# Four tokens of q and k per partition, permuted PSUM reads and contiguous writes in a chunked attention and wave-MLP kernel

## The chip, the cores and the metric

The kernel runs on one core of one Trainium2 chip. The core has five engines that run side by side: TensorE (PE in the profile, with its weight loads as PEld), VectorE (DVE), ScalarE (ACT), GpSimd (POOL, which here mostly issues loads) and SyncE (SP, which issues stores and transposing copies). Sixteen DMA engines move data between HBM and SBUF. The metric is the device time of one execution in microseconds; the time before is the median of 11 runs.

## The reference

q, k and v are 8 x 8 x 576 x 64 (batch, heads, tokens, head size). Attention is computed in chunks of 64 tokens; its output, with the heads side by side, is the input x (8 x 576 x 512) of a second phase.

```python
def attention(q, k, v):
    scores = scale * matmul(q_c, k_c.transpose(...))      # per chunk of 64 tokens
    attn = softmax(scores)
    out = matmul(attn, v_c)
    return out.reshape(B, H, S, D)

def wave_mlp(x, w_theta, w_tok_r, w_tok_i, w_ch):
    theta = x @ w_theta
    zr, zi = x * cos(theta), x * sin(theta)
    y = einsum('ts,bsd->btd', w_tok_r, zr) + einsum('ts,bsd->btd', w_tok_i, zi)
    u = x + y
    return u + maximum(u @ w_ch, 0.0)
```

## The kernel before

The eight batch rows are taken as four pairs of 1152 tokens, that is nine blocks of 128 tokens. A pair's blocks form five groups, `GROUPS` = (0,2), (2,2), (4,1), (5,2), (7,2): first block and number of blocks n. Group 2, the middle one, holds 64 tokens of either batch row; the other four are "large" (n = 2, 256 tokens) here and the middle one "small". All arithmetic is in fp16 with fp32 in PSUM; the loads convert from fp32.

There is no loop nest. `ORDER` is a list of items such as `a1.0.2:3`, written out by hand or by a planner, and the program walks it: the item's name picks a function, its numbers are pair, group and so on, and the number after the colon is a set of bits that choose engines and layouts. Each engine runs its instructions in the order in which this list produces them, and waits only on semaphores. The items are:

- `lq` (`load_qk`), `lv`, `lw`, `lt`, `lc`: loads, issued by POOL. Up to eight q/k tiles (`NAT`) are in flight or waiting. `lq` puts two tokens of a head side by side in a partition: a descriptor is 2 x 64 elements, 512 bytes in HBM and 256 in SBUF. A large group has 128 partitions x 8 heads of these for q and as many for k, in the same 128 partitions.
- `a1`: transposes q and k of a group on PE into one PSUM tile and copies q to `qT` and k to `kT` (`copy`, on ACT or DVE by bits 1 and 2). With bit 32 it uses 64 transposes of 64 rows, else 32 of 128 rows. The copies read PSUM in order; `kT` is written with its two tokens interleaved, so that keys stand in order of tokens.
- `a2`: scores, 64 x 64 each, on PE, then one exp on ACT that writes `eT` in order of query tokens, that is, every second element.
- `a3`: attention times v on PE, with the sums in a column of ones; reciprocal and product on DVE give x. `a4` transposes x (PE and a copy, or DMA with bit 16). `a5` is theta with its cosine and sine on ACT; `z` the products on DVE.
- `tw`: transposes of the token weights. `y`, `yh`: the token mixing, 18 matmuls and an addition on DVE. `ut`, `w`, `st`: the channel mixing, the final addition and the store, issued by SP or, with bit 2, by POOL.

PSUM holds four tiles of two banks each (`psum`, bufs=4), which all these stages share. `make_identity` is issued by POOL right after the first item. The transposes of `a1`, `a4` and `tw` need that identity.

Of the kernel before, what the change touches and what calls it, by code (L numbers as in the profile page):

```python
# [10 lines left out]
FP16 = mybir.dt.float16  # L11
# [5 lines left out]


ORDER = """
lq.0.0:0 lq.0.2:0 a1.0.0:35 a1.0.2:3 lq.0.1:0 a2.0.0:0 lv.0.2:0 a2.0.2:0 lv.0.0:0  # L20
a1.0.1:1 a3.0.2.0:0 a3.0.0.0:0 lw.0:0 lv.0.1:0 a3.0.0.1:0 a4.0.2:1 lq.0.3:0 a2.0.1:0
a4.0.0:33 a5.0.2:0 a3.0.1.0:0 a3.0.1.1:0 z.0.2.0:0 a5.0.0:0 lt.0.1:0 a4.0.1:33 a1.0.3:3
z.0.0.0:0 tw.0.0:1 lq.0.4:0 lt.1.0:0 tw.0.2:1 a5.0.1:0 lv.0.3:0 lt.1.1:0 z.0.0.1:0
lv.0.4:0 lq.1.0:0 z.0.1.0:0 z.0.1.1:0 lq.1.2:0 tw.0.1:1 a1.0.4:2 lq.1.1:0 a2.0.3:0
lv.1.2:0 tw.1.0:0 yh.0.0:0 a2.0.4:0 a3.0.3.0:0 lc.0:0 lv.1.0:0 a3.0.3.1:0 lq.1.3:0
yh.0.1:0 lq.1.4:0 tw.1.2:1 lv.1.1:0 lv.1.3:0 a4.0.3:1 lv.1.4:0 tw.1.1:1 a3.0.4.0:0
a3.0.4.1:0 a5.0.3:0 z.0.3.0:0 yh.1.0:0 a4.0.4:0 a1.1.0:1 a1.1.2:2 a5.0.4:0 z.0.3.1:0
lq.2.0:0 lq.2.2:0 z.0.4.0:0 yh.1.1:0 z.0.4.1:0 a2.1.2:0 a1.1.1:2 a2.1.0:0 w.0.0:0
lq.2.1:0 w.0.1:0 st.0.0:0 a2.1.1:0 st.0.1:0 y.0.1.0:0 a3.1.0.0:0 a3.1.2.0:0 a1.1.3:3
y.0.1.1:0 a4.1.2:0 a1.1.4:3 a2.1.3:0 a3.1.0.1:0 y.0.1.2:0 a3.1.1.0:0 a2.1.4:0 w.0.2:0  # L30
st.0.2:0 a5.1.2:0 a3.1.1.1:0 y.0.1.3:0 a4.1.1:0 a3.1.4.0:0 lv.2.3:0 a4.1.0:32 a1.2.0:35
w.0.3:0 z.1.2.0:0 a5.1.1:0 st.0.3:2 a3.1.3.0:0 a5.1.0:0 a3.1.4.1:0 lv.3.2:0 a1.2.2:2
a1.2.1:0 a3.1.3.1:0 a4.1.4:0 w.0.4:0 a4.1.3:0 lv.2.1:0 z.1.1.0:0 st.0.4:0 w.0.5:0
z.1.1.1:0 lq.2.3:0 z.1.0.0:0 a5.1.4:0 lv.2.0:0 w.0.6:0 st.0.5:2 z.1.0.1:0 a5.1.3:0
lq.2.4:0 lv.2.2:0 st.0.6:0 z.1.4.0:0 y.1.0.0:0 z.1.4.1:0 w.0.7:0 z.1.3.0:0 st.0.7:0
a1.2.3:35 a2.2.1:0 z.1.3.1:0 y.1.0.1:0 lq.3.0:0 w.0.8:0 lq.3.2:0 a2.2.0:0 st.0.8:2
lq.3.1:0 lv.2.4:0 lv.3.3:0 a2.2.2:0 y.1.0.2:0 a3.2.0.0:0 a3.2.2.0:0 y.1.0.3:0 a3.2.0.1:0
lv.3.4:0 a3.2.1.0:0 lq.3.3:0 y.1.1.0:0 a4.2.2:0 a2.2.3:0 a1.2.4:0 a3.2.1.1:0 w.1.0:0
lv.3.1:0 st.1.0:0 a5.2.2:0 a4.2.1:1 y.1.1.1:0 a4.2.0:32 a3.2.3.0:0 a1.3.0:35 a5.2.1:0
a1.3.2:2 z.2.2.0:0 lv.3.0:0 a3.2.3.1:0 a5.2.0:0 z.2.1.0:0 y.1.1.2:0 lq.3.4:0 a2.3.2:0  # L40
a2.2.4:0 z.2.0.0:0 z.2.1.1:0 a1.3.1:0 z.2.0.1:0 y.1.1.3:0 w.1.1:0 a3.2.4.0:0 st.1.1:0
ut.1.1.2:0 a3.3.2.0:0 y.2.0.0:0 a4.2.3:17 a2.3.0:0 a3.2.4.1:0 w.1.2:0 st.1.2:2 y.2.0.1:0
a2.3.1:0 a1.3.3:32 a4.2.4:16 a3.3.0.0:0 y.2.0.2:0 a2.3.3:0 a3.3.0.1:0 a1.3.4:35
y.2.0.3:0 a3.3.1.0:0 a2.3.4:0 ut.1.1.1:0 ut.1.1.0:0 ut.1.1.3:0 w.1.3:0 a5.2.3:0 w.1.4:0
w.1.5:0 st.1.3:2 st.1.4:2 st.1.5:2 a5.2.4:0 z.2.3.0:0 a3.3.1.1:0 z.2.4.0:0 w.1.6:0
z.2.3.1:0 a4.3.0:49 a5.3.0:0 ut.2.0.2:0 z.2.4.1:0 w.1.7:0 st.1.6:2 st.1.7:0 ut.2.0.1:0
y.2.1.0:0 a3.3.4.0:0 a4.3.2:51 a3.3.3.0:0 ut.2.0.3:0 y.2.1.1:0 ut.2.0.0:0 a3.3.4.1:0
a3.3.3.1:0 a4.3.1:49 y.2.1.2:0 w.1.8:0 st.1.8:0 a5.3.2:0 w.2.0:0 a4.3.3:17 st.2.0:2
y.2.1.3:0 a4.3.4:16 w.2.1:0 z.3.2.0:0 a5.3.1:0 z.3.0.0:0 st.2.1:0 w.2.2:0 z.3.0.1:0
st.2.2:2 ut.2.1.2:0 ut.2.1.3:0 z.3.1.0:0 ut.2.1.0:0 ut.2.1.1:0 a5.3.3:0 z.3.1.1:0  # L50
w.2.3:0 st.2.3:2 a5.3.4:0 z.3.3.0:0 y.3.0.0:0 z.3.4.0:0 z.3.3.1:0 w.2.4:0 st.2.4:0
y.3.0.1:0 ut.3.0.0:0 z.3.4.1:0 w.2.5:0 ut.3.0.1:0 y.3.0.2:0 w.2.6:0 st.2.5:2 ut.3.0.2:0
st.2.6:0 y.3.0.3:0 y.3.1.0:0 w.2.7:0 st.2.7:0 y.3.1.1:0 ut.3.0.3:0 w.2.8:0 st.2.8:2
y.3.1.2:0 y.3.1.3:0 ut.3.1.0:0 ut.3.1.1:0 w.3.0:0 w.3.1:0 st.3.0:2 st.3.1:2 w.3.2:0
w.3.3:0 w.3.4:0 st.3.2:2 ut.3.1.2:0 w.3.5:0 ut.3.1.3:0 st.3.3:0 w.3.6:0 st.3.4:0 w.3.7:0
st.3.5:0 st.3.6:2 w.3.8:0 st.3.7:0 st.3.8:0
""".split()


# [1 line left out]
def kernel(  # L61
# [11 lines left out]
    nc = tc.nc  # L73
    B, H, S, D = q.shape
    DM = H * D
    CH = 64
# [82 lines left out]

    def load_qk(p, g):  # L160

        j0, n = GROUPS[g]
        t = nat.tile([P, 2, H, 2, D], FP16, name="qk16")
        nats[p, g] = t
        for ti, ap in enumerate((q, k)):
            for pp, bb, s0, m in in_ranges(j0):
                m = n * m
                src = ap[2 * p + bb, :, s0 : s0 + m, :]
                nc.gpsimd.dma_start(  # L169
                    t[(pp // 2) : (pp // 2) + m // 2, ti].rearrange(  # L170
                        "p h t d -> p h (t d)"
                    ),
                    src.rearrange("h (p t) d -> p h (t d)", t=2),
                )

    def v_parts(p, g):
# [100 lines left out]
    def a1(p, g, bits):  # L277

        j0, n = GROUPS[g]
        ps = psum2("ps_qkT", FP16)  # L280
        if bits & 32:

            psv = ps.rearrange("p (r w e t s) -> p w e t r s", r=2, w=2, e=NE, t=2)
        else:
            psv = ps.rearrange("p (w e t r s) -> p w e t r s", w=2, e=NE, t=2, r=2)
        t = nats.pop((p, g))
        rows = n * CH
        step = CH if bits & 32 else rows
        for w in range(2):
            for e in range(NE):  # L290
                for tk in range(2):
                    for par in range(2):
                        for r0 in range(0, rows, step):
                            rs = slice(r0, r0 + step)
                            nc.tensor.transpose(  # L295
                                psv[par * D : par * D + D, w, e, tk,
                                    r0 // CH : (r0 + step) // CH, :],
                                t[rs, w, 2 * e + par, tk, :],
                                id16[rs, rs],
                            )  # L300

        qT = qkp.tile([P, NE, 2, P], FP16, name="qT")
        kT = qkp.tile([P, NE, P, 2], FP16, name="kT")
        st[p]["qkT"][g] = qT, kT
        copy(not bits & 1,
             qT[:, :, :, 0:rows].rearrange("p e t (r s) -> p e t r s", s=CH),
             psv[:, 0, :, :, 0:n])
        copy(bits & 2,
             kT[:, :, 0:rows, :].rearrange("p e (r s) t -> p e t r s", s=CH),
             psv[:, 1, :, :, 0:n])  # L310

    def a2(p, g):

        j0, n = GROUPS[g]
        qT, kT = st[p]["qkT"].pop(g)
        kT = kT.rearrange("p e s t -> p e (s t)")

        ps = psum2("ps_sT").rearrange("p (r x) -> p r x", r=2)[:, :, 0 : n * NE * CH]
# [1 line left out]
        for i in range(n):  # L320
            for e in range(NE):
                for par in range(2):
                    for kh in range(2):
# [1 line left out]
                        nc.tensor.matmul(  # L325
                            psv[kh * CH : kh * CH + CH, par, i, e, :],
                            kT[par * D : par * D + D, e, c0 : c0 + CH],
                            qT[par * D : par * D + D, e, :, c0 // 2 : (c0 + CH) // 2],
                        )

        eT = epool.tile([P, 2 * H * CH], FP16, name="eT")[:, 0 : n * H * CH]
        st[p]["eT"][g] = eT.rearrange("p (r i e c) -> p r i e c", r=2, i=n, e=NE)
        nc.scalar.activation(  # L333
            out=eT.rearrange("p (r b s t) -> p r b t s", r=2, s=CH // 2, t=2),
            in_=ps.rearrange("p r (b t s) -> p r b t s", s=CH // 2, t=2),
            func=AF.Exp,
            scale=scale,
        )

    def a3(p, g, hg):  # L340

# [302 lines left out]
```

## Time and profile before

| what | us |
|---|---|
| median of 11 runs | 204.22 |
| lowest, highest | 202.84, 205.14 |
| profiled execution | 204.0 |
| its span | 202.2 |
| PE busy in the span | 185.0 |
| DVE busy | 129.2 |
| ACT busy | 108.5 |
| POOL busy | 94.8 |

The profile shows one execution. Its own time, 204.0, is 1.8 us above the span, which runs from the first to the last instruction. Durations from it are set against this execution. In a group's line, the numbers after the count are the busy time, the mean of one instruction in ns and, after the bar, the idle time of the engine just before with what ended it. "128*64" on a PE line means that 128 rows and 64 columns of the array are used. PE's ends are modelled, so that starts of successive instructions tell more than its busy share.

### The profile page before, as it was taken

The page shows a single profiled execution, that of the slowest core. Times are in us where ns is not written, and L with a number is a line of the kernel's source. Part 1 is how long each engine was busy: PE and PEld are TensorE (multiplying, and loading weights), DVE is VectorE, ACT ScalarE, POOL GpSimd, SP SyncE. Part 2 cuts the span into 40 slices and gives each one's busy share as a digit, 9 for nine tenths or more (in the row PEclk, how much of TensorE's full clock was granted, in tenths as well). Part 3 has the DMA queues.
Part 4 walks back from the last instruction along what each step waited for, and adds up shares of the span by engine and source line. Part 5 has one row for each costly group of instructions (what it writes and reads, how often), then busy time and mean ns, then how long its engine had stood idle before and what let it go on. Part 6 is the DMA issues. An engine that isn't in the chain of part 4 may idle for free.

```text
span 202.2 us, 7044 instructions
## 1 busy us (share of the span) xinstructions
PE 185.0 (91%) x3142; PEld 124.5 (62%) x3142; DVE 129.2 (64%) x224; ACT 108.5 (54%) x114; POOL 94.8 (47%) x135
## 2 busy tenths in 40 slices
PE   0377999999999998999999899999999999999991
PEld 0265377776677746567777477775466646677640
DVE  1037669836777669667685887565868494544572
ACT  2068499499826877969159792665841265000000
POOL 7989639798596108994599620101310111011020
PEclk9999999999999999999999999999999999999999
DMA  6999999999999907999999992746744659482786
GB/s 144 165 162 171 187 194 167 177 180 173 171 220 175 167 16 103 123 219 210 227 154 153 156 161 63 146 86 92 206 140 99 182 144 198 100 160 79 156 276 216
DMA packets 102157, 31.96 MB, mean 158 GB/s; under 512 B 95792, under 2 KB 98480, under 8 KB 102128
## 3 DMA queue, kind: packets, MB, share of 16 engines
q0 software_dynamic: 78800, 20.70, 98.0%
q1 hardware_dynamic: 23328, 10.82, 23.0%
q8 instruction: 24, 0.39, 0.8%
q14 instruction: 5, 0.04, 0.1%
HBM read 33.06 MB, written 9.44 MB: 210 GB/s over the span
## 4 chain that ended last, share of the span: by engine, by line
PE 75%; ACT 8%; DMA 6%; DVE 6%; issue 2%; POOL 1%; DVEq 0%; POOLq 0%
PE ps_y L521 30%; PE ps_uw L560 15%; PE ps_theta L443 13%; PE ps_qkT L295 4%; PE ps_y L500 3%; DMA qk<-in_k_dram 3%; PE ps_x L354 3%; DMA v<-in_v_dram 2%; PE ps_sT L325 2%; PE ps_xT L417 2%; ACT qT L214 2%; DVE x L368 2%; DVE kT L212 2%; ACT eT L333 1%; ACT xT L214 1%
## 5 line engine op out<-in xcount | busy, mean ns | idle before, releaser
L521 PE MATMUL ps_y<-wT,z 128*128 128x288 f16 x448 | 59.6, 287 | 0.5 <-PE ps_theta L443 0.5
L521 PEld LDWEIGHTS <-z 128*128 128x128 f16 x448 | 42.4, 98 | 13.8 <-PE ps_theta L443 1.0
L598 POOL DMA_DIRECT2D out_dram<-o x18 | 9.9, 552 | 82.6 <-DVE o L589 49.4
L190 POOL DMA_DIRECT2D v<-in_v_dram x56 | 41.9, 771 | 10.6 <-DMA qk<-in_k_dram 6.1
L560 PE MATMUL ps_uw<-wch,uT 128*128 128x512 f16 (+1 forms) x148 | 37.6, 374 | 0.0
L529 DVE TENSOR_TENSOR uT<-ps_y,xT 128x576 f16<-128x576 f32 x28 | 21.2, 756 | 24.7 <-PE ps_y L521 24.7
L443 PE MATMUL ps_theta<-wtheta,xT 128*128 128x512 f16 x128 | 31.7, 393 | 0.1
L453 ACT ACTIVATE cos<-ps_theta,pihalf 128x1024 f16<-128x1024 f32 (+1 forms) x20 | 20.6, 1029 | 16.5 <-PE ps_theta L443 14.7
L333 ACT ACTIVATE eT<-ps_sT 128x1024 f16<-128x1024 f32 (+1 forms) x20 | 23.5, 1200 | 10.5 <-PE ps_sT L325 10.5
L295 PE MATMUL ps_qkT<-id,qk 64*64 64x64 f16 (+1 forms) x832 | 20.2, 214 | 8.6 <-DMA qk<-in_q_dram 6.8
L368 DVE TENSOR_TENSOR x<-ps_x,recip 128x512 f16<-128x512 f32 x36 | 24.9, 692 | 1.2
L212 DVE COPY kT<-ps_qkT 128x1024 f16<-128x1024 f16 (+1 forms) x14 | 15.8, 1137 | 12.7 <-ACT qT L214 12.7
L295 PEld LDWEIGHTS <-qk 64*64 64x64 f16 (+1 forms) x832 | 17.3, 115 | 10.5 <-DMA qk<-in_q_dram 7.3
L560 PEld LDWEIGHTS <-uT 128*128 128x128 f16 x148 | 14.4, 98 | 14.2
L169 POOL DMA_DIRECT2D qk<-in_q_dram x24 | 19.7, 826 | 3.8 <-DMA qk<-in_q_dram 1.9
L169 POOL DMA_DIRECT2D qk<-in_k_dram x24 | 19.1, 799 | 4.3 <-DMA qk<-in_q_dram 2.5
L443 PEld LDWEIGHTS <-xT 128*128 128x128 f16 x128 | 12.2, 100 | 14.4 <-issue 1.6
L589 DVE SCALAR_TENSOR_TENSOR o<-ps_uw,un 128x512 f32<-128x512 f32 (+1 forms) x24 | 15.8, 667 | 5.3 <-PE ps_uw L560 3.8
L457 ACT ACTIVATE sin<-ps_theta 128x1024 f16<-128x1024 f32 (+1 forms) x20 | 18.6, 931 | 0.0
L214 ACT COPY qT<-ps_qkT 128x1024 f16<-128x1024 f16 (+1 forms) x11 | 10.7, 976 | 11.6 <-PE ps_qkT L295 11.5
L468 DVE TENSOR_TENSOR z<-x,cos 128x1024 f16<-128x1024 f16 x16 | 11.0, 686 | 4.2 <-ACT cos L453 4.0
L585 DVE TENSOR_TENSOR o<-ps_uw,o 128x512 f32<-128x512 f32 x13 | 9.0, 690 | 7.0 <-ACT o L576 7.0
(54 smaller groups left out, 196.3 us busy)
## 6 DMA issues: line engine op xcount, KB each, us to landing
qk<-in_q_dram POOLq DMA_DIRECT2D x16, 256.0 KB, 6.2
qk<-in_k_dram POOLq DMA_DIRECT2D x16, 256.0 KB, 6.8
out_dram<-o POOLq DMA_DIRECT2D x16, 256.0 KB, 3.0
out_dram<-o SPq DMA_DIRECT2D x15, 256.0 KB, 2.8
v<-in_v_dram POOLq DMA_DIRECT2D x40, 64.0 KB, 5.9
v<-in_v_dram POOLq DMA_DIRECT2D x16, 128.0 KB, 5.6
out_dram<-o SPq DMA_DIRECT2D x8, 128.0 KB, 2.3
tok<-in_moe_w_tok_r_dram SPq DMA_DIRECT2D x1, 576.0 KB, 3.6
```

The costliest lines, as they stand in the source:

```text
L169: nc.gpsimd.dma_start(t[(pp // 2) : (pp // 2) + m // 2, ti].rearrange("p h t d -> p h (t d)"), src.rearrange("h (p t) d -> p h (t d)", t=2),)
L190: nc.gpsimd.dma_start(v16[pp : pp + m, sl, :, 0:D], v[2 * p + bb, :, s0 : s0 + m, :].rearrange("h s d -> s h d"),)
L212: nc.vector.tensor_copy(out=out, in_=in_)
L295: nc.tensor.transpose(psv[par * D : par * D + D, w, e, tk, r0 // CH : (r0 + step) // CH, :], t[rs, w, 2 * e + par, tk, :], id16[rs, rs],)
L333: nc.scalar.activation(out=eT.rearrange("p (r b s t) -> p r b t s", r=2, s=CH // 2, t=2), in_=ps.rearrange("p r (b t s) -> p r b t s", s=C ...
L368: nc.vector.tensor_tensor(out=xo, in0=px[:, :, :, 0:D], in1=recip.broadcast_to((P, 2, NE, D)), op=ALU.mult,)
L443: nc.tensor.matmul(ps[:, jj * DM : jj * DM + DM], xt[:, db, :], wtheta16[:, db, :], start=(db == 0), stop=(db == NDB - 1),)
L453: nc.scalar.activation(out=cos[:, 0:n].rearrange("p a e -> p (a e)"), in_=pin, func=AF.Sin, bias=pihalf, scale=1.0,)
L457: nc.scalar.activation(out=sin[:, 0:n].rearrange("p a e -> p (a e)"), in_=pin, func=AF.Sin)
L521: nc.tensor.matmul(psv[:, hf, 0:HS], zt[:, db * P : db * P + P], wT[:, kt, hf * HS : hf * HS + HS], start=(kt == 0), stop=(kt == 2 * KT),)
L529: nc.vector.tensor_tensor(out=uT_tile(p)[:, db, sl].rearrange("p (f c) -> p f c", f=2), in0=psv[:, :, 0:HS], in1=xT_tile(p)[:, db, sl].rea ...
L560: nc.tensor.matmul(out, uT[:, db, j * P : j * P + P], wch16[:, db, cols], start=(db == 0), stop=(db == NDB - 1),)
```

## The change

For a large group, `load_qk` puts four tokens of a head side by side (`tk = 2 * n`): descriptors of 1 KB in HBM and 512 bytes in SBUF, 64 partitions x 8 heads for q in partitions 0 to 63 and as many for k in partitions 64 to 127. The small group keeps two tokens and uses 32 + 32 partitions for q and as many for k. `a1` makes every transpose from 64 rows, alternating between q (upper rows, first bank) and k (lower rows, second bank). `qT` keeps the order of PSUM; `kT` and exp now read PSUM permuted and write in order. For the small group exp becomes two instructions. `a2` takes its queries as four runs of 16 instead of two of 32 (large groups). `ORDER` is new from end to end, with its bits; the items are the same. The bit 32 of `a1` is gone.

```diff
 ORDER = """
-lq.0.0:0 lq.0.2:0 a1.0.0:35 a1.0.2:3 lq.0.1:0 a2.0.0:0 lv.0.2:0 a2.0.2:0 lv.0.0:0
-a1.0.1:1 a3.0.2.0:0 a3.0.0.0:0 lw.0:0 lv.0.1:0 a3.0.0.1:0 a4.0.2:1 lq.0.3:0 a2.0.1:0
-a4.0.0:33 a5.0.2:0 a3.0.1.0:0 a3.0.1.1:0 z.0.2.0:0 a5.0.0:0 lt.0.1:0 a4.0.1:33 a1.0.3:3
...
-w.3.3:0 w.3.4:0 st.3.2:2 ut.3.1.2:0 w.3.5:0 ut.3.1.3:0 st.3.3:0 w.3.6:0 st.3.4:0 w.3.7:0
-st.3.5:0 st.3.6:2 w.3.8:0 st.3.7:0 st.3.8:0
+lq.0.2:0 lq.0.0:0 a1.0.2:0 lq.0.1:0 lv.0.0:0 tw.0.0:0 lv.0.2:0 a2.0.2:0 a1.0.0:1
+lq.0.3:0 a1.0.1:1 a2.0.0:0 a3.0.2.0:0 a2.0.1:0 a1.0.3:1 a4.0.2:1 a3.0.0.0:0 lv.0.1:0
+a3.0.1.0:0 a2.0.3:0 lw.0:0 a3.0.0.1:0 a3.0.1.1:0 lv.0.3:0 a5.0.2:0 lt.0.1:0 lq.0.4:0
...
+ut.3.1.1:0 ut.3.1.2:0 st.3.1:2 ut.3.1.3:0 w.3.4:0 st.3.2:2 w.3.5:0 w.3.6:0 st.3.3:2
+st.3.4:0 st.3.5:0 st.3.6:0 w.3.7:0 w.3.8:0 st.3.7:0 st.3.8:0
 """.split()
...
     def load_qk(p, g):
         j0, n = GROUPS[g]
-        t = nat.tile([P, 2, H, 2, D], FP16, name="qk16")
+        tk = 2 * n
+        t = nat.tile([P, H * 4 * D], FP16, name="qk16")[:, 0 : H * tk * D]
+        t = t.rearrange("p (h t d) -> p h t d", h=H, t=tk)
...
+                r0 = ti * CH + pp // 2
                 nc.gpsimd.dma_start(
-                    t[(pp // 2) : (pp // 2) + m // 2, ti].rearrange(
-                        "p h t d -> p h (t d)"
-                    ),
-                    src.rearrange("h (p t) d -> p h (t d)", t=2),
+                    t[r0 : r0 + m // tk].rearrange("p h t d -> p h (t d)"),
+                    src.rearrange("h (p t) d -> p h (t d)", t=tk),
                 )
...
     def a1(p, g, bits):
-        for w in range(2):
-            for e in range(NE):
-                for tk in range(2):
-                    for par in range(2):
-                        for r0 in range(0, rows, step):
-                            rs = slice(r0, r0 + step)
-                            nc.tensor.transpose(
-                                psv[par * D : par * D + D, w, e, tk,
-                                    r0 // CH : (r0 + step) // CH, :],
-                                t[rs, w, 2 * e + par, tk, :],
-                                id16[rs, rs],
-                            )
...
-        copy(not bits & 1,
-             qT[:, :, :, 0:rows].rearrange("p e t (r s) -> p e t r s", s=CH),
-             psv[:, 0, :, :, 0:n])
-        copy(bits & 2,
-             kT[:, :, 0:rows, :].rearrange("p e (r s) t -> p e t r s", s=CH),
-             psv[:, 1, :, :, 0:n])
+        psv = ps.rearrange("p (w x) -> p w x", w=2)[:, :, 0 : NE * n * P]
+        psv = psv.rearrange("p w (e t s) -> p w e t s", e=NE, t=tk)
+        for e in range(NE):
+            for ti in range(tk):
+                for par in range(2):
+                    for w in range(2):
+                        rs = slice(w * CH, w * CH + CH)
+                        nc.tensor.transpose(
+                            psv[par * D : par * D + D, w, e, ti, :],
+                            t[rs, 2 * e + par, ti, :],
+                            id16[rs, rs],
+                        )
...
+        copy(not bits & 1, qv, psv[:, 0])
+        copy(bits & 2, kv, psv[:, 1].rearrange("p e t s -> p e s t"))
 
     def a2(p, g):
...
-                            qT[par * D : par * D + D, e, :, c0 // 2 : (c0 + CH) // 2],
+                            qT[par * D : par * D + D, e, :, c0 // tk : (c0 + CH) // tk],
...
-        nc.scalar.activation(
-            out=eT.rearrange("p (r b s t) -> p r b t s", r=2, s=CH // 2, t=2),
-            in_=ps.rearrange("p r (b t s) -> p r b t s", s=CH // 2, t=2),
-            func=AF.Exp,
-            scale=scale,
-        )
+        eo = eT.rearrange("p (r x) -> p r x", r=2)
+        for out, in_ in (
+            [(eT, ps.rearrange("p r x -> p (r x)"))] if n == 2
+            else [(eo[:, r], ps[:, r]) for r in range(2)]
+        ):
+            nc.scalar.activation(
+                out=out.rearrange("p (b s t) -> p b s t", s=CH // tk, t=tk),
+                in_=in_.rearrange("p (b t s) -> p b s t", s=CH // tk, t=tk),
+                func=AF.Exp,
+                scale=scale,
+            )
```

## The prediction

> **What bounds the kernel now.** I read the page's shares and slices first, then the chain that ended last, then the busy time of each engine by stage, then the groups with shapes kept apart.
>
> ```profile
> PE 185.0 (91%) x3142; PEld 124.5 (62%) x3142; DVE 129.2 (64%) x224; ACT 108.5 (54%) x114; POOL 94.8 (47%) x135
> ...
> PE   0377999999999998999999899999999999999991
> ...
> ACT  2068499499826877969159792665841265000000
> ...
> PE 75%; ACT 8%; DMA 6%; DVE 6%; issue 2%; POOL 1%; DVEq 0%; POOLq 0%
> ```
>
> TensorE (PE) holds three quarters of the chain. After its first 20 us it is busy in nearly every slice, while ACT and DVE never fill for long. The chain in order of time shows both ends of the story: the start belongs to DMA, the rest to PE.
>
> ```profile
> 2.31 6.71 DMA qk<-in_k_dram
> ...
> 11.32 4.99 DMA v<-in_v_dram
> ...
> 21.60 3.29 PE ps_theta L443 x8
> ...
> 90.19 0.64 PE ps_qkT L295 x64
> ...
> 103.56 1.01 PE ps_qkT L295 x32
> ...
> 113.29 1.90 PE ps_theta L443 x8
> ```
>
> q/k, then v, gate the first 16 us. Two more things are to be seen. Eight theta matmuls take 3.29 us at 21.60 but 1.7 to 1.9 later, so PE runs at half pace until about 24.5 us. And a transpose of one q/k group costs 1.01 us as 32 transposes of 128 rows, but 0.64 us as 64 transposes of 64 rows.
>
> ```profile
> 20.00:30.00 10.00, 10.00 (x159) 5.41 (x159) 6.08 (x12) 7.05 (x10) 5.58 (x9) 1.00 1.65 191
> 30.00:40.00 10.00, 9.59 (x223) 7.54 (x218) 8.91 (x16) 7.41 (x8) 8.38 (x12) 1.00 1.80 172
> ...
> 70.00:80.00 10.00, 9.48 (x262) 6.11 (x258) 8.09 (x18) 7.51 (x9) 3.20 (x5) 1.00 0.33 60
> ...
> 110.00:120.00 10.00, 9.42 (x236) 6.17 (x223) 8.34 (x17) 8.62 (x9) 5.53 (x7) 1.00 1.79 162
> ```
>
> Columns after the stretch: PE, PE weight load, DVE, ACT, POOL, granted clock, DMA share, GB/s. Over the stretches from 20 to 190 us the idle time of PE adds to 2.0 us (0.41 + 0.52 + 0.15 + 0.58 + 0.35). That is the most that faster evictions alone can give there.
>
> ```profile
> L333 ACT ACTIVATE eT<-ps_sT 128x1024 f16<-128x1024 f32 x16 | 21.0, 1314 | 10.5 <-PE ps_sT L325 10.5
> ...
> L457 ACT ACTIVATE sin<-ps_theta 128x1024 f16<-128x1024 f32 x16 | 16.3, 1017 | 0.0
> ...
> L212 DVE COPY kT<-ps_qkT 128x1024 f16<-128x1024 f16 x10 | 13.0, 1304 | 12.7 <-ACT qT L214 12.7
> ...
> L214 ACT COPY kT<-ps_qkT 128x1024 f16<-128x1024 f16 x6 | 7.9, 1313 | 2.1 <-DVE qT L212 2.1
> ```
>
> The exp and the kT copies write every second element; the sine of the same size, written contiguously, is 297 ns cheaper.
>
> [...]qT on DVE takes 684 ns, the strided kT 1304. [...]No row of this trace reads PSUM element by element at size, nor loads a 64-partition q. [...]
>
> **The change, part by part.**
> *PE transposes.* Of the sixteen two-block groups, ten are now 32 transposes of 128 rows and six are 64 of 64 rows. All become 64 of 64 rows[...]: 1.01 to 0.64, 0.37 us less for each of ten. One (13.13 us) lies in the DMA-gated start and gives nothing: 9 x 0.37 = 3.3 us. The four one-block groups keep 32 transposes[...]. They take about 0.45 now (the 1.64 us pair of groups at 43.76 less 1.01, less a pause before it of 0.15) and an estimated 0.33 then, half of 64 transposes: 3 x 0.12 = 0.35 us. Against this, three x-transposes go from 32 small to 8 large ones, 0.41 to 0.45 in the chain: 0.1 us. [...]Net PE: -3.5 us, nearly all inside the PE-held part.
>
> *Evictions.* exp and kT now write contiguously and read PSUM in steps. If the read is free, exp goes from 1314 to 1017: 16 x 0.297 = 4.8 us off ACT. The four 512-element exps become eight of 256: 154 ns fixed + 0.84 per element (from the 512 and 1024 copies, 585 and 1016) is 0.37 each, 0.74 a pair, as now (0.742). kT on ACT goes from 6 x 1.31 to 7 x 1.02 + 2 x 0.59. With the other copies moved by the new order (two more large and two more small qT, two large xT and two large wT fewer) ACT falls from 108.5 to about 104 us. DVE keeps kT at 1.22 to 1.30 (the lower value: uT, 576 elements in 756 ns, gives 1024 elements in about 1.22) and falls to about 127. None of this is the bound, so it is worth a part of the 2.0 us of idle PE: bounds 0 and -2.0, I take -0.5. The unknown is the permuted read: from 0 to, at worst, a doubling (1.017 to 1.9 us, 0.55 above today's exp). I take zero, since ACT takes 1024 elements from PSUM in the same time in fp32 (sin, 1017 ns) and in fp16 (qT, 1016), so it seems to be held by elements, not by bytes.
>
> *Loads.* For each of the sixteen large groups q and k need 2 x 512 descriptors in place of 2 x 1024, of 1 KB, into 64 partitions each. POOL's DMA queue takes 98% of the engines' time over the span, but no PE wait after 16.4 us is on a DMA, so later loads are hidden. The cover is the prefetch through eight buffers, unchanged; [...]So loads are 0 to 20% faster, not slower.
>
> *Order, start.* The order is new throughout. The small group comes first. POOL issues four small q/k loads (1.54 + 1.14 us in the trace), the identity, then the large ones; the first transpose can start near 6.5 us against 6.85, with wT's first eight behind it. The set needed for the first attention-times-v is the same 2.24 MB (tok, three q/k, two v); it landed at 16.4 us. But now q/k of group 3 and v of group 1 (768 KB) stand on POOL's queue ahead of w_theta, which landed at 19.0 (issued at 12.2, 6.8 to land). At 165 GB/s w_theta would come at 23.6; with the lighter descriptors nearer 21.5. While it waits PE has other work drawn forward: q/k transposes and scores of group 3, v products of group 1, the first wT, together some 1.8 us at full clock; before, PE used 19 to 24 us for twelve cold theta matmuls worth 2.6 us at full clock. ACT's list is longer too before its first cosine: four more copies of about 1 us. Bounds for the start: -2.5 us (loads 20% faster over 14 us) to +3 (theta late and everything behind it). I take +0.5.
>
> *Tail.* The last 40 theta-sized w matmuls (7.8 us), DVE's o and the stores are the same. Three un transposes (1.27 us each on SP) and the last stores, one of which went out by POOL, now follow each other on SP's queue; a store takes SP 0.35 us against 0.86 us of matmul per tile. Zero.
>
> *Sum.* The profiled execution took 204.0 us (span 202.2). 204.0 - 3.5 - 0.5 + 0.5 = 200.5. The median of the runs, 204.22, is 0.2 above, within their scatter; I forecast 200.5.
>
> **Rivals.**
> *A, late start.* theta waits for w_theta[...]: +2.5 in place of +0.5, 202.5. For it: w_theta comes 4.6 us later by bytes, and nothing on POOL's queue overtakes. Against: fewer descriptors, more PE work in front.
> *B, early start.* Loads by descriptors, not bytes: -2 at the start, -1 for evictions: 204.0 - 3.5 - 3 = 197.5. For it: DMA saturated from the first slice.[...]
> *C, moved wait.* PE gets faster in stages where ACT (9.0 of 10 at 40 to 50, 8.6 at 110 to 120) or DVE (8.9 at 30 to 40) is nearly full, and PE waits instead: the 3.3 us of the nine groups come back as idle time, 203.8, no change. Against: ACT gets 4 us lighter.
> *D, slower: the permuted read of PSUM.* At double price every exp and kT gains 0.55 us over today: (16 + 7) x 0.55 + 8 x 0.2 = 14 us on ACT, 9 x 0.5 = 4.5 on DVE. ACT is busy 99 of the 140 us from 10 to 150; in the dense stages it has 1 to 2 us free in ten, so I count half as PE waits: +7 - 3.5 = 207.5. It turns the result once a 1024-element read passes about 1.6 us, where half the added ACT and DVE time equals the 3.5 us.[...]
>
> **How the numbers follow.** Forecast (199 to 202) 0.46; A 0.14; B 0.13; C 0.09; D 0.18. A measurement of this kernel tells 0.3%, 0.6 us, from no change. Faster: 0.46 + 0.14 + 0.13 = 0.73; within 0.3%: 0.09; slower: 0.18. The range 196.8 to 205.2 takes in B, the forecast, A and C and leaves out D (0.18) and little more; the forecast's own range is 199 to 202.
>
> **What would show it.** Right: every full q/k transpose group at 0.64 to 0.70 us and PE busy time down by 3 to 4 us; exp at about 1017 ns and kT on ACT at 1016; kT on DVE no lower than 1.2; half the packets for the sixteen large loads. The first theta between 20 and 23 us tells A from the forecast. Wrong: exp above 1.6 us (D); PE idle over 4 us between 25 and 190 us (C); transposes of 64 rows that stay near 1 us[...].

## The result, and the profile after

The change is slower. The median of 12 runs after it is 206.64 us, of the kernel before on the same chip 203.86 us; the ratio is 1.0135 with a 95% interval of 1.011 to 1.0159. The profiled execution took 207.25 us with a span of 205.5 us, against 204.0 and 202.2 before. All ratios here leave out executions over 1.5% above the fastest of their kernel; this matters most for one kernel below, `late_split_2`, of whose six executions three remain (206.03 to 208.8 us) and whose profile, at 210.41 us, is not one of these.

The first lines are from the page of the kernel after: busy time by engine, the slices of TensorE and its granted clock, two DMA queues (packets, MB, share of the engines' span), and the shares of the chain that ended last.

```profile
PE 181.6 (88%) x3390; PEld 121.6 (59%) x3390; DVE 126.3 (61%) x220; ACT 104.4 (51%) x122; POOL 88.8 (43%) x136
...
PE   0554579798999999999999999999999999999992
...
PEclk9999999997999999999999999999999999999999
...
q0 software_dynamic: 62496, 20.96, 86.6%
...
q8 instruction: 26, 0.43, 0.9%
...
PE 74%; ACT 7%; DMA 7%; DVE 5%; issue 5%; POOL 2%; DVEq 0%; POOLq 0%
```

TensorE has 3.4 us less to do (185.0 before), ACT 4.1 and DVE 2.9. The span is 3.3 us longer all the same, so TensorE idles 6.7 us more. "issue", time in which an engine waited for nothing that the profile shows, has grown from 2% to 5% of the chain. The busy time by stretch (stretch; PE, PEld, DVE, ACT and POOL busy; clock; DMA share; GB/s) says where. The first two lines are after the change, the last two before it.

```profile
0.00:60.00 60.00, 41.12 (x1064) 29.13 (x1065) 28.49 (x55) 36.02 (x41) 46.79 (x73) 0.97 1.57 172
60.00:120.00 60.00, 59.11 (x1311) 40.67 (x1309) 40.91 (x73) 38.47 (x48) 32.69 (x47) 1.00 1.35 161
...
0.00:60.00 60.00, 48.90 (x1013) 34.55 (x1014) 34.06 (x60) 38.21 (x39) 48.75 (x70) 1.00 1.72 176
60.00:120.00 60.00, 58.75 (x1225) 40.34 (x1223) 43.68 (x80) 44.21 (x49) 37.89 (x51) 1.00 1.52 156
```

The whole deficit of TensorE, 7.8 us (48.90 less 41.12), arises in the first 60 us. The chain of the kernel after, in order of time (start, us, what), shows its start.

```profile
5.99 5.82 DMA qk<-in_q_dram
...
12.09 7.62 DMA qk<-in_k_dram
...
21.77 2.02 issue
...
25.24 1.89 PE ps_theta L445 x4
...
31.22 1.74 PE ps_theta L445 x8
```

Loads of q and k hold the chain until 19.7 us. After 2 us of TensorE's work comes a hole of 2.02 us that belongs to no transfer and no engine, and the first theta starts at 25.2 us (19.1 before). The unit prices, on the other hand, are those that were forecast. These lines are from the groups after, with shapes kept apart.

```profile
L293 PE MATMUL ps_qkT<-id,qk 64*64 64x64 f16 x1152 | 16.4, 206 | 10.4 <-DMA qk<-in_q_dram 6.4 <-DMA qk<-in_k_dram 3.7 <-issue 0.3
L335 ACT ACTIVATE eT<-ps_sT 128x1024 f16<-128x1024 f32 x16 | 16.3, 1025 | 22.7 <-PE ps_sT L321 22.7
...
L214 DVE COPY kT<-ps_qkT 128x1024 f16<-128x1024 f16 x9 | 11.0, 1222 | 10.4 <-ACT qT L216 10.4
...
L216 ACT COPY kT<-ps_qkT 128x1024 f16<-128x1024 f16 x7 | 7.1, 1018 | 1.6 <-DVE qT L214 1.6
```

So the loss lies in something that the sum had no term for, in the order, or in both.

### The profile page after: what moved, and what is told of

Same layout as the page of the kernel before. It is cut to its first block, busy times and chain, and to the rows that moved or that the text cites. A ratio compares the mean times of both kernels' runs of the same rounds, so it can differ in the third digit from the quotient of the medians.

```text
span 205.5 us, 7536 instructions
## 1 busy us (share of the span) xinstructions
PE 181.6 (88%) x3390; PEld 121.6 (59%) x3390; DVE 126.3 (61%) x220; ACT 104.4 (51%) x122; POOL 88.8 (43%) x136
## 4 chain that ended last, share of the span: by engine, by line
PE 74%; ACT 7%; DMA 7%; DVE 5%; issue 5%; POOL 2%; DVEq 0%; POOLq 0%
PE ps_y L523 30%; PE ps_uw L562 16%; PE ps_theta L445 14%; PE ps_qkT L293 4%; DMA qk<-in_k_dram 4%; PE ps_x L356 3%; DMA qk<-in_q_dram 3%; PE ps_xT L419 3%; DVE kT L214 2%; ACT qT L216 2%; ACT sin L459 2%; POOL qk L173 2%; ACT cos L455 2%; PE ps_sT L321 2%; PE ps_uw L570 1%
## 5 line engine op out<-in xcount | busy, mean ns | idle before, releaser
L523 PEld LDWEIGHTS <-z 128*128 128x128 f16 x448 | 42.7, 98 | 13.6 <-DVE x L370 0.5
L335 ACT ACTIVATE eT<-ps_sT 128x1024 f16<-128x1024 f32 (+1 forms) x24 | 18.7, 810 | 23.3 <-PE ps_sT L321 23.2
L445 PE MATMUL ps_theta<-wtheta,xT 128*128 128x512 f16 x128 | 30.1, 381 | 0.4 <-DVE xT L214 0.4
L455 ACT ACTIVATE cos<-ps_theta,pihalf 128x1024 f16<-128x1024 f32 (+1 forms) x20 | 20.6, 1031 | 11.3 <-PE ps_theta L445 9.0
L370 DVE TENSOR_TENSOR x<-ps_x,recip 128x512 f16<-128x512 f32 x36 | 24.9, 692 | 1.2
L293 PE MATMUL ps_qkT<-id,qk 64*64 64x64 f16 x1152 | 16.4, 206 | 10.4 <-DMA qk<-in_q_dram 6.4
L293 PEld LDWEIGHTS <-qk 64*64 64x64 f16 x1152 | 13.8, 117 | 13.6 <-DMA qk<-in_q_dram 7.1
L214 DVE COPY kT<-ps_qkT 128x1024 f16<-128x1024 f16 (+1 forms) x11 | 12.4, 1124 | 10.7 <-ACT qT L216 10.7
L459 ACT ACTIVATE sin<-ps_theta 128x1024 f16<-128x1024 f32 (+1 forms) x20 | 18.7, 934 | 0.0
L173 POOL DMA_DIRECT2D qk<-in_q_dram x24 | 16.6, 695 | 4.4 <-DMA wtheta<-in_moe_w_theta_dram 1.6
L173 POOL DMA_DIRECT2D qk<-in_k_dram x24 | 15.9, 667 | 4.7 <-DMA qk<-in_q_dram 2.1
L216 ACT COPY qT<-ps_qkT 128x1024 f16<-128x1024 f16 (+1 forms) x15 | 13.9, 927 | 7.2 <-PE ps_qkT L293 7.2
L356 PE MATMUL ps_x<-v,eT 64*64 64x65 f16 x576 | 12.2, 204 | 5.8 <-DMA v<-in_v_dram 2.6
L356 PEld LDWEIGHTS <-eT 64*64 64x64 f16 x576 | 8.7, 115 | 11.3 <-issue 7.7
```

The lines of the kernel that those rows point to most:

```text
L173: nc.gpsimd.dma_start(t[r0 : r0 + m // tk].rearrange("p h t d -> p h (t d)"), src.rearrange("h (p t) d -> p h (t d)", t=tk),)
L293: nc.tensor.transpose(psv[par * D : par * D + D, w, e, ti, :], t[rs, 2 * e + par, ti, :], id16[rs, rs],)
L335: nc.scalar.activation(out=out.rearrange("p (b s t) -> p b s t", s=CH // tk, t=tk), in_=in_.rearrange("p (b t s) -> p b s t", s=CH // tk, ...
L356: nc.tensor.matmul(psv[half * CH : half * CH + CH, kh if n == 2 else f0, cols], eT[kh * CH : kh * CH + CH, h % 2, i, h // 2, :], v16[kh * ...
L370: nc.vector.tensor_tensor(out=xo, in0=px[:, :, :, 0:D], in1=recip.broadcast_to((P, 2, NE, D)), op=ALU.mult,)
L445: nc.tensor.matmul(ps[:, jj * DM : jj * DM + DM], xt[:, db, :], wtheta16[:, db, :], start=(db == 0), stop=(db == NDB - 1),)
```

## The experiments

Fifteen kernels were run, each timed against the kernel before on the same chip. "Old" and "new" are the two `ORDER` lists, "halves" is a 64-row transpose of q or k alone, "whole" a 128-row one. "Listed" counts TensorE's matmuls and transposes in the trace (some records can be missing); each has a weight load beside it.

| run | functions | order | listed | first theta, us | median, us | ratio (95%) |
|---|---|---|---|---|---|---|
| after | new | new | 3390 | 25.2 | 206.64 | 1.0135 (1.011 to 1.0159) |
| order_only | before | new | 2878 | 25.1 | 210.22 | 1.0309 (1.0258 to 1.0361) |
| code_only | new | old | 3462 | 19.4 | 213.74 | 1.0486 (1.043 to 1.0541) |
| evict_only | before, new reads and writes | old | 3142 | 18.7 | 203.54 | 0.9979 (0.9956 to 1.0002) |
| head_old | new | mixed | 3438 | 19.7 | 215.01 | 1.0522 (1.0467 to 1.0577) |
| all_split | before, all large groups in halves | old | 3462 | 19.1 | 211.87 | 1.0358 (1.031 to 1.0406) |
| none_split | before, all large groups whole | old | 2950 | 19.4 | 205.50 | 1.0086 (1.0058 to 1.0114) |
| few_old | new, all whole | old | 2886 | 21.6 | 205.58 | 1.0087 (1.0053 to 1.012) |
| mix_old | new, six groups in halves | old | 3078 | 19.3 | 203.75 | 0.9979 (0.9953 to 1.0006) |
| few_new | new, all whole | new | 2814 | 24.3 | 209.84 | 1.0319 (1.0278 to 1.036) |
| start_whole_2 | new, pair 0 whole | new | 3246 | 24.9 | 207.32 | 1.0171 (1.0119 to 1.0223) |
| late_split_2 | new, pairs 0 and 1 whole | old | 3174 | 20.4 | 209.14 | 1.018 (1.0111 to 1.025) |
| head_whole | new, all whole | mixed | 2862 | 21.5 | 214.21 | 1.0509 (1.046 to 1.0559) |
| loads_old | new, all whole | new, loads in the old sequence | 2814 | 27.6 | 215.83 | 1.0575 (1.0541 to 1.0609) |
| loads_new | new, all whole | old, loads in the new sequence | 2886 | 24.7 | 215.07 | 1.0544 (1.0504 to 1.0584) |
| change_loads_old | new | new, loads in the old sequence | 3390 | 27.2 | 211.36 | 1.0365 (1.0332 to 1.0397) |

### Taking the change apart

Four kernels: the new order with the functions of before, the new functions with the old order, the evictions alone, and the new functions under an order whose items ahead of the first `yh` stand in the old sequence.

```diff
 ORDER = """
-lq.0.0:0 lq.0.2:0 a1.0.0:35 a1.0.2:3 lq.0.1:0 a2.0.0:0 lv.0.2:0 a2.0.2:0 lv.0.0:0
+lq.0.2:0 lq.0.0:0 a1.0.2:0 lq.0.1:0 lv.0.0:0 tw.0.0:0 lv.0.2:0 a2.0.2:0 a1.0.0:1
...
```

> The functions of before under the new order. Theory O: the loss of about 6.5 us at the head without the gain of the code, 209 to 211 us, first y near 41. Theory L: the new order suits the old loads no worse than the new ones, 203 to 206, first y before 36.

> The changed functions (loads, transposes, evictions) under the order of before. Theory O (the loss lies in the new order, whose head feeds TensorE later): the code's own gain shows, 3.5 us of transposes and up to 0.5 of evictions, so 199.5 to 201 us where before takes 203.9; first theta near 19 us, first y near 32. Theory L (the 64-partition loads of 1 KB feed the start no faster or later, whatever the order): 203.5 to 206, q/k tiles landing later than in before, first theta after 21 us.

> The changed kernel with the items that stand ahead of its first y put into before's order among themselves; everything after keeps the new order. Theory O with the head as the place: first theta at 19 to 21 us instead of 25, most of the 6 us come back, 200 to 203. If the order's later part is at fault: 205.5 to 207. Theory L: 205.5 to 207 too, with q/k landings that stay late.

The evictions alone, in the kernel before:

```diff
+        kv = kT[:, :, 0:rows, :].rearrange("p e (r s) t -> p e r s t", s=CH)
...
+                copy(bits & 2, kv[:, :, r],
+                     psv[:, 1, :, :, r].rearrange("p e t s -> p e s t"))
...
-            out=eT.rearrange("p (r b s t) -> p r b t s", r=2, s=CH // 2, t=2),
-            in_=ps.rearrange("p r (b t s) -> p r b t s", s=CH // 2, t=2),
+                out=out.rearrange("p (b s t) -> p b s t", s=CH // 2, t=2),
+                in_=in_.rearrange("p (b t s) -> p b s t", s=CH // 2, t=2),
```

> Before, with permuted PSUM reads and contiguous writes alone (two tokens, old order; the six groups with 64-row transposes need two kT copies each). Theory O and the prediction's sum: exp 1314 to about 1025 ns, and the time moves by 0 to -1 us, since TensorE holds the path: 203 to 204. If ACT held the path more than the chain showed: 201 or less.

The evictions do what was forecast: 0.4 us, at the edge of what can be told. From the groups of that run:

```profile
L347 ACT ACTIVATE eT<-ps_sT 128x1024 f16<-128x1024 f32 x16 | 16.4, 1024 | 12.1 <-PE ps_sT L334 12.0
```

The other three are surprises. The order alone costs 6.3 us, the functions alone 9.8 us, the two together only 2.8. An explanation by the order alone, or by its head, cannot stand: the new functions are slow in the old order, and slower still with an old head. The timeline of TensorE in the run with the new functions and the old order (start, us, what, idle time before in brackets) has the clue.

```profile
63.20 0.45 PE L293 MATMUL ps_qkT<-id,qk 64*64 64x64 f16 x32
66.57 0.44 PE L293 MATMUL ps_qkT<-id,qk 64*64 64x64 f16 x32 [2.93 <-issue]
```

This is one group of 64 transposes. Both its operands are there since its first transpose started, its PSUM tile is its own, and yet TensorE stops for 2.93 us half way, waiting for nothing that the profile shows. No missing operand explains that. Whether missing instructions do is tried next.

### Is it the fetch of instructions?

Theory F: TensorE outruns the fetch of its own instructions. The rival, L: the 64-partition loads land later. Four kernels, all under the old order. The first two leave the loads as they were and change only the number of transposes, by the bit 32 of each `a1`:

```diff
 ORDER = """
-lq.0.0:0 lq.0.2:0 a1.0.0:35 a1.0.2:3 lq.0.1:0 a2.0.0:0 lv.0.2:0 a2.0.2:0 lv.0.0:0
-a1.0.1:1 a3.0.2.0:0 a3.0.0.0:0 lw.0:0 lv.0.1:0 a3.0.0.1:0 a4.0.2:1 lq.0.3:0 a2.0.1:0
+lq.0.0:0 lq.0.2:0 a1.0.0:35 a1.0.2:35 lq.0.1:0 a2.0.0:0 lv.0.2:0 a2.0.2:0 lv.0.0:0
+a1.0.1:33 a3.0.2.0:0 a3.0.0.0:0 lw.0:0 lv.0.1:0 a3.0.0.1:0 a4.0.2:1 lq.0.3:0 a2.0.1:0
...
```

> The kernel before with its loads, its layout, its writes and its order, but the transposes of all sixteen large groups cut into 64-row halves (six are in the kernel before). That gives TensorE the instruction count of the run with the new functions under the old order, 3462 listed transposes and matmuls against 3142, and takes 10 x 0.37 = 3.7 us of transposes away. Theory F (TensorE outruns the fetch of its own instructions, which come in 16 KB packets of a queue of their own, when it eats them at 10 ns each in a stretch where the loads fill the DMA engines): 207 to 213 us, with pauses of 1 to 3 us in the middle of groups of transposes that end about 1.4 us after such a packet has landed. Theory L (the 64-partition loads of 1 KB descriptors land later, or with the wrong group first): no such loads here, so 199 to 202 us.

> The kernel before with the transposes of all large groups of 128 rows: 192 listed instructions fewer, and 6 x 0.37 = 2.2 us more of transposes. Theory F: what the kernel before itself loses to the fetch is small (no pause over 1 us in its trace), so 204 to 206 us, no pause over 1 us behind a packet. Theory L says the same; the run is the other end of the scale for the count of instructions, and tells how much of the added transpose time reaches the end.

The other two keep the new loads, reads and writes, and transpose q and k of a token together, in all groups or in all but the six that are in halves before:

```diff
+        psv = ps.rearrange("p (x w s) -> p x w s", w=2, s=CH)[:, 0 : NE * tk]
+        psv = psv.rearrange("p (e t) w s -> p w e t s", e=NE)
         for e in range(NE):
             for ti in range(tk):
                 for par in range(2):
-                    for w in range(2):
-                        rs = slice(w * CH, w * CH + CH)
-                        nc.tensor.transpose(
-                            psv[par * D : par * D + D, w, e, ti, :],
-                            t[rs, 2 * e + par, ti, :],
-                            id16[rs, rs],
-                        )
+                    nc.tensor.transpose(
+                        psv[par * D : par * D + D, :, e, ti, :],
+                        t[:, 2 * e + par, ti, :],
+                        id16,
+                    )
```

> The new functions under the old order, but with one transpose for each token of both q and k (q in rows 0 to 63 and k in rows 64 to 127, so 128 rows into 64 partitions of PSUM): 32 transposes for a large group, 16 for a small one, where the change has 64 and 32. Loads, layout, permuted reads and contiguous writes are those of the change. Against the run with the new functions under the old order (213.7 us) TensorE does 16 x 0.37 = 5.9 us more of transposes and 576 fewer of them. Theory F: the pauses go, 203 to 207 us, faster than that run in spite of the added work. Theory L: the loads are the same, so the waits on them stay, and the time is 213.7 or more.

> As the run before, but the six large groups that the kernel before transposes in halves are transposed in halves here too: the loads, layout, reads and writes of the change, with the transpose time and (but for 64 in the small groups) the instruction count of the kernel before, under its order. Theory F: 202 to 205 us, as the kernel before less up to half a us for the evictions. Theory L: 208 us or more, with TensorE waiting on q and k.

F holds and L falls. Halves in all large groups cost the kernel before 3.6% although they take work away (TensorE busy 181.7 us against 185.0). The same loads as in the change cost nothing when the transposes are few or as before: 205.6 and 203.75 us. With all groups whole, few_old and none_split agree within 0.1 us.

The timeline of TensorE with all groups in halves, a kernel in which not one load is changed:

```profile
118.76 0.56 PE L295 MATMUL ps_qkT<-id,qk 64*64 64x64 f16 x24
121.74 0.25 PE L295 MATMUL ps_qkT<-id,qk 64*64 64x64 f16 x4 [2.41 <-issue]
```

TensorE stops after 24 transposes of a group, in the middle of q. What the DMA engines did while it stood, from the DMA view of that run between 119.1 and 120.2 us (packets, MB, share):

```profile
q0 software_dynamic: 714, 0.18, 168.7%
q8 instruction: 1, 0.02, 5.1%
```

One packet of the queue called "instruction" passes among 714 of loads. That queue is TensorE's: the number of its packets, of 16,384 bytes each, goes up and down with TensorE's instructions from run to run, while the only other instruction queue has 5 packets in every run.

```profile
q8 instruction: 24, 0.39, 0.8%
```

This line is the page of the kernel before, which lists 2 x 3142 instructions on TensorE: 262 for each of 24 packets. With all groups in halves it is 2 x 3462 for 27 (256 each), with all whole in the new functions 2 x 2886 for 22 (262). So a packet is a block of about 256 instructions, 128 matmuls with their weight loads; the second and the last pause below lie 1913 matmuls apart, which is 15 blocks of 127.5. The six longest pauses just after such a packet in the run with all groups in halves, from the records of the trace:

| packet landed, us | matmuls started before the pause | pause from start to start, us | TensorE resumed after the landing, us |
|---|---|---|---|
| 13.81 | 209 = 1 x 128 + 81 | 0.99 | 1.33 |
| 26.33 | 477 = 3 x 128 + 93 | 1.50 | 1.49 |
| 32.88 | 604 = 4 x 128 + 92 | 1.55 | 1.52 |
| 57.83 | 1114 = 8 x 128 + 90 | 1.39 | 1.48 |
| 64.15 | 1242 = 9 x 128 + 90 | 2.87 | 1.63 |
| 120.10 | 2390 = 18 x 128 + 86 | 2.60 | 1.64 |

The first row may not belong here: a load of v landed 0.04 us before TensorE resumed, and the profile puts that wait down to it. The other five lie a whole number of blocks apart, to within a few matmuls and whatever the group (two of them stop matmuls of theta and y), and end 1.5 to 1.6 us after a packet has landed. The run with the new functions and the old order, in which the same items have the same counts, has its two longest pauses at the same two matmuls, 1242 (3.12 us from start to start) and 2390 (2.86 us). The five add to 9.9 us; less 3.3 us of work saved, that is 6.6 of the 8.4 us by which this span (210.6) exceeds that of before.

The records also say what is late: the start of the packet, not its transfer. In this run no packet starts before TensorE is at matmul 66 of the block before it, and the five pauses come at matmul 86 to 93 of the next block, some 150 matmuls later. From that matmul 66, or from the landing of the packet before where that is later, 15 packets start only after 2.5 to 5.6 us, 4.2 in the median; these are the ones where the loads' queue moved more than 100 GB/s in the 2 us before the packet and during it. The other 12 start after 0.0 to 3.4 us, 1.2 in the median. The transfer takes about 1.0 us in both. So beside loads a block needs, as an estimate from these medians, 4.2 + 1.0 + 1.5 = 6.7 us from that point until TensorE goes on. Where TensorE has done its 150 matmuls sooner, it stops: in the five cases it came to the end of them 4.0 to 6.5 us after that point.

So a crossing from one block to the next can show: five of them cost 1.4 to 2.9 us each here. In the run with the new functions and the old order the granted clock falls to 0.87 between 60 and 70 us, behind the pause of 2.93 us. Of the four pauses over 2.5 us in this run and the one with all groups in halves, three are followed by 3.4 us at a granted clock of 0.5. Where a pause brings that about it is paid for again; that it does is not shown.

That the loads' traffic is what delays the packet's start was not tried by itself: no run took the loads away. It rests on the two medians above.

### And the change's own order?

In the trace of the change TensorE stops twice in the start, for 2.58 us at 14.5 us and for 2.25 us at 21.5 us, from start to start; during each stop such a packet landed, at 15.65 and 22.26 us, 1.5 us before TensorE resumed. These are the matmuls behind the two stops (start, us, what, idle time before).

```profile
17.11 0.26 PE L356 MATMUL ps_x<-v,eT 64*64 64x65 f16 x1 [2.34 <-DMA v<-in_v_dram]
...
23.78 0.43 PE L356 MATMUL ps_x<-v,eT 64*64 64x65 f16 x14 [2.02 <-issue]
```

The second is the hole in the chain. The first, which the expectations below count as a pause for instructions too, ended 0.04 us after a load of v had landed, so it may be a wait for v; that a block was late as well can't be told apart. Is the late start the doing of these two? One kernel transposes pair 0 whole, another everything whole; both keep the new order.

```diff
+        if p > 0:
+            psv = ps.rearrange("p (w x) -> p w x", w=2)[:, :, 0 : NE * n * P]
+            psv = psv.rearrange("p w (e t s) -> p w e t s", e=NE, t=tk)
...
+                    if p == 0:
+                        nc.tensor.transpose(
+                            psv[par * D : par * D + D, :, e, ti, :],
+                            t[:, 2 * e + par, ti, :],
+                            id16,
+                        )
+                        continue
```

> The change with its own order, all groups transposed whole (32 transposes for a large group, 16 for a small one), so that with the old-order run of the same functions (205.6 us) the order is compared where no pause for instructions is in play. Theory F with an order that costs nothing of itself: 205 to 206.5 us. With an order that costs of itself (the functions of the kernel before took 210.2 us in it, and 205.5 us in the old order with the same whole transposes): 208 to 211 us.

> The change with its own order, but the five groups of the first pair (p = 0) are transposed whole, q and k of a token together by one 128-row transpose; the other pairs keep the 64-row halves. 288 transposes fewer than in the change, all before 30 us, and 4 x 0.37 = 1.5 us more of transposes there. Theory F alone (the change's late start is TensorE waiting for its instructions): the pauses of 2.58 us at 14.5 us and of 2.25 us at 21.5 us go, the first theta matmul comes at 20 to 23 us instead of 25.2, and the time is 201.5 to 204.5 us, at or below the kernel before. Theory F with an order that starts late of itself (with all groups whole, first theta is still at 24.3 us in the new order against 21.6 us in the old one, and the time 209.8 against 205.6 us): first theta 24 to 25 us, 204.5 to 207.5 us, since the pauses only fill time in which TensorE would have waited.

It is not. With the first pair whole the two stops are gone (a gap of 1.1 us that ends with the next transposes at 20.6 us is put down to k), and the first theta is at 24.9 us, the time 207.3. The waits of TensorE in that run (line and what it waited for: us in total, times, longest):

```profile
PE ps_qkT L295 <- DMA qk<-in_k_dram: 11.6, 4, 6.3
PE ps_sT L331 <- ACT kT L216: 2.2, 3, 1.2
PE ps_wT L235 <- DVE kT L214: 1.7, 2, 1.1
```

Time that the stops had filled goes to waits on k: in this order TensorE stands there anyway. And with everything whole the new order takes 209.8 us where the old one takes 205.6, 4.2 us more; with the functions of before, which have no group in halves under the new order, it is 210.2 against 205.5, 4.7 us more. So the order costs 4.2 to 4.7 us of itself. With everything whole, the new order has no pause for instructions over 0.9 us, and its clock does not fall before the end. But first theta is at 24.3 us against 21.6, and TensorE is busy less between 40 and 50 us. The first line is the old order, the second the new one.

```profile
40.00:50.00 10.00, 9.81 (x144) 6.61 (x141) 5.64 (x11) 7.59 (x9) 8.11 (x12) 1.00 1.52 160
...
40.00:50.00 10.00, 8.60 (x210) 6.53 (x207) 6.07 (x11) 7.13 (x9) 7.87 (x12) 1.00 1.71 174
```

With the functions of before and everything whole, TensorE is busy 49.0 of the first 60 us in the old order and 45.8 in the new one, so 3.2 of the 4.7 us arise there.

Which part of the order is it? Three kernels keep the compute items of one order and put the loads in the sequence of the other; a fourth mixes the head.

```diff
 ORDER = """
-lq.0.2:0 lq.0.0:0 a1.0.2:0 lq.0.1:0 lv.0.0:0 tw.0.0:0 lv.0.2:0 a2.0.2:0 a1.0.0:1
+lq.0.0:0 lq.0.2:0 a1.0.2:0 lq.0.1:0 lv.0.2:0 tw.0.0:0 lv.0.0:0 a2.0.2:0 a1.0.0:1
...
```

> The new functions with all groups transposed whole, in the new order, but the loads stand in the old order's sequence in the slots that the new order has for loads (three of them pulled ahead to the item that needs them): first q and k of group 0, then of group 2, v of group 2 ahead of group 0, w_theta sixth instead of eighth. New order throughout 209.8 us, old order throughout 205.6 us. Theory P (the new order costs by its sequence of loads: v of group 2 fifth, w_theta eighth, first theta at 24.3 us): first theta at 20 to 22.5 us, 205 to 207.5 us. Theory Q (it costs by its sequence of compute items): 208.5 to 211 us.

> The counterpart: the same functions in the old order, with the loads in the new order's sequence in the old order's slots. Theory P: first theta at 23 to 25 us, 208 to 210.5 us. Theory Q: 205 to 207 us.

> The whole change, 64-row halves throughout, in its own order, with the loads in the old order's sequence as in the first of these three runs. Theory P: 202.5 to 205 us, less than the change's 206.6, if no pause for instructions longer than 2 us comes in. Theory Q: 206 to 209 us.

> The new functions with all groups transposed whole, so that no pause for instructions is in play, under a mixed order: what the new order has ahead of the first y half (about 55 items, up to some 40 us) stands in the old order's sequence, all that follows in the new one's. Between 205.6 us (old order throughout) and 209.8 us (new order throughout). If the 4.2 us of the order are its head, with first theta at 24.3 us: first theta at 21 to 22 us and 205 to 207 us. If they are in the rest: first theta at 21 to 22 us and still 208.5 to 211 us.

None of these expectations came in. With everything whole each mixture takes 214 to 216 us, more than either order; the change with the loads in the old sequence takes 211.4 us against its own 206.6. The waits of TensorE with the new compute order and the old loads, then with the old compute order and the new loads:

```profile
PE ps_qkT L291 <- DMA qk<-in_k_dram: 13.8, 2, 11.1
```

```profile
PE ps_qkT L291 <- DMA qk<-in_k_dram: 11.0, 1, 11.0
PE ps_x L354 <- DMA v<-in_v_dram: 4.4, 2, 2.9
PE ps_theta L443 <- DMA wtheta<-in_moe_w_theta_dram: 2.2, 1, 2.2
```

In both, the first group to be transposed is the second to be loaded, so TensorE begins at 11 us. A part of the loss can be the clock, which the expectations had no term for. This is the granted clock by slices of the new order with the old loads.

```profile
PEclk9998576999999999999999999999999999999999
```

Between the start and the end it stands at half for 13.6 us in this run and in `head_whole`, for 10.2 us in the old order with the new loads and for 6.8 us in the change with the old loads, against 0 and 6.8 us in the new and the old order with everything whole and 3.4 us in the change. In the change's 3.4 us (48.5 to 52.0 us) transposes of x start 107 ns apart, from there on 56. So half of such a time, 6.8, 5.1 and 3.4 us for the four mixtures, is an estimate of the most that it costs. So the swap of one sequence doesn't price the other. What in the new order costs the 4.2 us stays open.

### Is there a better version?

The last kernel puts the halves where the run with all of them had fewest pauses, in pairs 2 and 3 under the old order.

```diff
+        if p > 1:
+            psv = ps.rearrange("p (w x) -> p w x", w=2)[:, :, 0 : NE * n * P]
...
+                    if p < 2:
...
```

> The loads, layout, permuted reads and contiguous writes of the change under the old order; pairs 0 and 1 transposed whole, pairs 2 and 3 in halves (eight large groups in halves where the kernel before has six). TensorE does 0.7 us less of transposes than in the kernel before, and the evictions on ScalarE are some 5 us shorter in sum. Theory F: 202 to 203.5 us, below the kernel before, if no block of instructions is late in pairs 2 and 3; with one pause of 2.6 to 2.9 us as at 119 us in the runs with all groups in halves under this order, 204.5 to 206 us.

It is slower, by a ratio of 1.018, and missed both expectations. The execution that was profiled, the longest of the six, has two pauses at a block's end, 2.08 us at 113.6 and 2.78 us at 119.8: those pairs too still have loads beside them. Whether the shorter executions have these pauses is not shown. The best runs, the evictions alone and the new functions with six groups in halves, have a ratio of 0.9979 and intervals that reach 1.

## Why the prediction was wrong

It forecast 200.5 us, 196.8 to 205.2; measured were 206.64. A ladder of runs that change one part at a time gives the sum that should have stood there: from 203.9 us, +1.7 for the new functions with every group whole (205.6: 2.2 us more of transposes, less some for the evictions), +4.2 for the new order (209.8), -3.2 for cutting all groups in halves (206.6). Together +2.7. The ladder holds for this sequence of steps alone: under the old order the last step costs 8.2 us (205.6 to 213.7).

- *PE transposes, "Net PE: -3.5 us, nearly all inside the PE-held part".* This step failed in its conclusion, not in its prices. Large groups take 0.64 to 0.70 us and TensorE's busy time fell by 3.4. But the step counted durations only. It never counted instructions, and the profile page of before had the queue that brings them, with 24 packets. Cutting the last ten large groups in halves, alone and in the old order, was to give -3.7 and gave +7.9. Under the new order, where TensorE waits for k and v in the start anyway, halves gave -3.2 where 16 x 0.37 = 5.9 were priced. The trace of the change has the pause of 2.25 us, and a granted clock of 0.93 and 0.90 between 40 and 60 us where it is 1.00 with everything whole.
- *Order, start, "I take +0.5", bounds -2.5 to +3.* This term was mis-sized. Measured with every group whole the order costs 4.2 to 4.7, above the upper bound, and this is the larger of the two misses. The place, the first 60 us, was right; that the later theta behind more loads is what costs it is not shown. The text had split it into the landing of `w_theta` and other work drawn forward. First theta came at 24 to 25 us in every pure run of that order, with w_theta the last wait in the run with the functions before (its transfer is in the chain from 16.71 to 25.01 us) but not in the change.
- *Evictions, -0.5.* Right as far as can be told: -0.4 measured, with an interval that reaches no change, exp at 1025 ns, kT at 1018 on ACT and 1222 on DVE. On ACT the permuted read of PSUM costs nothing that shows (kT 1018 ns, qT read in order 1016 before), and on DVE kT is no slower than before (1304), so rival D fell with its premise, a double price that was the author's own bound; the case was slower, but not by its mechanism.
- *Loads, "0 to 20% faster, not slower", hidden.* Half right. The 20%, which the bound of -2.5 for the start took over, was the author's estimate: no load of q or k of before went into 64 partitions. The loads are hidden: with the transposes as before, the new loads leave the time where it was (203.75). They are hardly faster: the large loads' packets halve (32,768 of 256 bytes in SBUF, then 16,384 of 512), but the transfers run at 170 GB/s from 10 to 15 us and 180 from 15 to 20 after, against 162 and 172 before, 5% more. With the new loads under the old order (`mix_old`, `few_old`, `code_only`) they run at 158 to 170 and 168 to 180, so the 5% is within the scatter. Bytes decide more than descriptors here, which takes rival B away too.
- *Rivals A and C.* A, the late start, had the place and the sign, at +2.5. C's mark, TensorE idle over 4 us between 25 and 190 us, is there (4.9 us, 2.0 before). 4.0 of it lies before 60 us, and 3.2 of that ends with work of DVE, 2.1 with kT copies. So C's wait is there in part, but not its reason: DVE is busy 6.0 to 6.7 us of each 10 in these stretches and ACT 6.1 to 7.5, so neither is full. None of the rivals was the fetch.
- *Tail, zero.* No run tested it by itself. From 120 to 190 us TensorE is busy 70.0 of 70 us (69.65 before).

## What to carry to other kernels

Before cutting an operation into more and shorter ones, count the instructions per microsecond that the engine will have to be fed (for a group here, with the weight loads, 128 in 0.64 us or 64 in 1.01 us), and look for the instruction queue in the list of DMA queues: five pauses here, some in the middle of a group whose operands were all there, lay a multiple of 128 matmuls apart and ended 1.5 to 1.6 us after a packet of that queue had landed. The order here was fitted to its loads as a whole: none of five mixtures of the two orders came out as its halves would have it. So a new order should be taken as an unknown with a wide price. And run the order and the code apart: here the two together (+2.8 us) hid that each alone was worse.

## What the runs showed of the hardware

- TensorE's instructions come in packets of 16,384 bytes, about 256 instructions (24 packets for 6284 before), by a DMA queue of their own. With all groups in halves, a packet beside loads of over 100 GB/s started 4.2 us in the median after the earliest point seen, the others 1.2 us; TensorE resumed 1.5 to 1.6 us after the landing of a late one. The pauses reached 2.9 us there and 3.1 us with the new functions and the old order.
- On ACT an exp of 1024 elements takes 1025 ns with a permuted read of PSUM and a contiguous write, 1314 with a read in order and a write of every second 16-bit element; a sine with neither takes 1017. Copies of kT take 1018 and 1313 in these two forms, of qT, with neither, 1016. So on ACT it is that write that cost, not the permuted read. On DVE kT takes 1222 ns against 1304 in the same two forms, and qT, with neither, 684 before.
- Loads into 64 partitions in 512-byte pieces move about as fast as into 128 in 256-byte pieces: in the stretches from 10 and from 15 us, 170 and 180 GB/s in the change and 158 to 170 and 168 to 180 in three runs under the old order, against 162 and 172 before.
